# Sums of squares mostly in bf16 instead of fp32, evenly spaced covariance units and a relu square moved back to VectorE, in a fused attention and channel-mix kernel

## Chip, cores and metric

One core of a Trainium2 chip. The metric is the device time of one execution in microseconds (us). PE is the matrix engine, VectorE is DVE, ScalarE is ACT and GpSimd is POOL in the profile.

## The reference

Four batches of 6208 rows and 256 channels. A cross-covariance attention runs over the channels, and a channel mix follows it.

```python
qn = q / (norm(q, axis=1) + 1e-6);  kn = k / (norm(k, axis=1) + 1e-6)
a = softmax(kn.T @ qn / tau)               # 256 x 256 per batch
x = v @ a                                  # 6208 x 256
xk = mu_k*x + (1-mu_k)*x_prev;  xr = mu_r*x + (1-mu_r)*x_prev
out = sigmoid(xr @ w_r) * (maximum(xk @ w_k, 0)**2 @ w_v)
```

The norms need the column sums of q² and k² over all rows of a batch.

## The kernel before

The program is emitted in a fixed order, eight steps `j` for each of 48 blocks of 512 rows (12 blocks a batch). While the blocks of one batch go through the channel mix, the covariance of the next batch is made in between, in *units* of 128 rows. A unit is two matmuls, and every second unit has one ScalarE square of the q and k rows; the last unit of a batch has 64 rows. The squares are added up on VectorE. Each add is queued at build time and emitted at one of three places in a block (steps 1, 6 and 7; at step 2 too while a softmax chain waits for its sums).

Names in the views: `delta`, `xk` and `xr` mix each row with the one before it; `kr` is the relu and `kk` its square; `vr_ps` is the PSUM buffer of the last matmuls of 128 rows, and `res` the step that reads and frees it; `sq` and `acc` are squares and their sums, and `bank` holds the norms.

```python
def unit_square(b, g, s):                  # two rows (s, s+1) of a group of four
    ...
    t = pq.tile([P, 2, 2 * C], F32, name="sq2", ...)
    adds.append((now[0] + 2, b, t))
    if apart(b, g):                        # batch 1: q and k lie apart, two squares
        for i in range(2):
            nc.scalar.activation(t[:rows, :, i * C:(i + 1) * C], rows_at(qk, b, g, i)[:rows, s:s + 2], AF.Square)
    else:
        nc.scalar.activation(t[:rows], qk[...], AF.Square)

def next_add():
    _, b, t = adds.pop(0)
    nc.vector.tensor_tensor(sums[b], sums[b], t, op=OP.add)     # 128 x 1024 fp32
...
# up(): relu of each of 8 tiles on ScalarE; in blocks 1-33 ScalarE also squares the first of them
if fh == 0 and by_act(i):
    nc.scalar.activation(st[i, "kk"][:, 0, :m], kr, AF.Square)
...
# finish(): frees vr_ps, of which there are two
nc.scalar.activation(res[:, s], vr_ps[:, D:], AF.Tanh, scale=0.5)
nc.vector.scalar_tensor_tensor(res[:, s], res[:, s], 1.0, vr_ps[:, :D], op0=OP.add, op1=OP.mult)
...
# the block loop: the steps j that take a unit
elif i < 7:
    slots = (1, 2, 3, 4, 5, 7) if i < 3 else (1, 2, 3, 4, 5, 6, 7)
elif i == 7:
    slots = (1, 2, 7)
elif (i - 7) % NB == 0:
    slots = (5, 7)
else:
    slots = (1, 3, 4, 5, 7) if (i - 7) % NB in (1, 3, 6, 9) else (1, 3, 5, 7)
if j in slots and pos["mm"] < len(units):
    unit()
if adds and adds[0][0] <= now[0] and (j in (1, 6, 7) or j == 2 and adds[0][1] == holds[0] and chain):
    next_add()
```

After a batch's last unit comes its softmax `chain`, one piece a step. It holds the norms (small matmuls on the sums) back until all adds of that batch have been emitted.

Of the kernel before, what the change touches and what calls it, by code (L numbers as in the profile page):

```python
# [18 lines left out]
def kernel(  # L19
# [13 lines left out]
    nc = tc.nc  # L33
# [173 lines left out]
    def unit_square(b, g, s):  # L207

        rows, n = rows_of(b, g)
        if s % 2:  # L210
            return
        qk = groups[b, g][0]
        if n == 1:
            t = pq.tile([P, 1, 2 * C], BF16, name="sq", tag="sq1", bufs=2)
            sums[b, "left"] = t
        elif (g, s) == (1, 0):
            t = pn.tile([P, 2, 2 * C], F32, name="acc", tag="acc", bufs=2)
            sums[b] = t
        else:
            t = pq.tile([P, 2, 2 * C], F32, name="sq2", tag=f"f{s // 2}", bufs=6)  # L220
            adds.append((now[0] + 2, b, t))
        if apart(b, g):
            for i in range(2):
                nc.scalar.activation(t[:rows, :, i * C:(i + 1) * C], rows_at(qk, b, g, i)[:rows, s:s + 2], AF.Square)
        else:
            nc.scalar.activation(t[:rows], qk[:rows, s:s + min(n, 2)].rearrange("p s i c -> p s (i c)"), AF.Square)  # L226

    def next_add():
        _, b, t = adds.pop(0)
        nc.vector.tensor_tensor(sums[b], sums[b], t, op=OP.add)  # L230

    def unit_matmul(b, g, s):
        rows, n = rows_of(b, g)
# [11 lines left out]
    def softmax_pieces(b):  # L245

        s_ps = cov.pop(b) if b else None
        rn = pn.tile([P, 4], F32, name="rn")
        s_sb = pn.tile([P, 2, C], F32, name="s_sb")
        e_sb = pn.tile([P, 2, C], F32, name="e_sb", bufs=1)  # L250
        mx = pn.tile([P, 2], F32, name="mx")
        sm = pn.tile([P, 2], F32, name="sm")
        rk = rn[:, 2:4]
        def fold():
            t = pq.tile([P, 2 * C], BF16, name="sq", tag="sq", bufs=1)
            nc.vector.tensor_tensor(t, sums[b][:, 0], sums[b][:, 1], op=OP.add)
            sums[b] = t

        def norms():
            bank[b] = ps.tile([P, 4], F32, name="bank", tag="xT_ps", bufs=2)  # L260
            for t, rows in ((sums.pop((b, "left"))[:, 0], L), (sums.pop(b), P)):
                for i in range(4):
                    nc.tensor.matmul(bank[b][:, i:i + 1], t[:rows, i * P:(i + 1) * P], ones[:rows, 0:1],
                                     start=rows == L and i == 0, stop=rows == P, skip_group_check=True)

        def roots():
            nc.scalar.copy(rn, bank[b])

        def diagonals():
            dg = pn.tile([P, 2, P], F32, name="dg", tag="dg", bufs=1)  # L270
            for h in range(2):
                nc.vector.tensor_tensor(dg[:, h], cov[0][h][:, 3 * P * h:3 * P * h + P], ident_f, op=OP.mult)
            nc.vector.tensor_reduce(rn[:, 0:2], dg, axis=AX, op=OP.add)

        def root(h):
            nc.scalar.activation(rn[:, 2 * h:2 * h + 2], bank[0][:, 0:2] if h else rn[:, 0:2], AF.Sqrt)

        def invert_first(h):
            nc.vector.tensor_scalar_add(rn[:, 2 * h:2 * h + 2], rn[:, 2 * h:2 * h + 2], 1e-6)
            nc.vector.reciprocal(rn[:, 2 * h:2 * h + 2], rn[:, 2 * h:2 * h + 2])  # L280
            if h and inv_tau != 1.0:
                nc.vector.tensor_scalar_mul(rk, rk, inv_tau)

        def evac_first():
            for h in range(2):
                nc.vector.tensor_scalar_mul(s_sb[:, h], cov[0][h][:, P:P + C], rn[:, h:h + 1])

        def pow2():
            nc.gpsimd.tensor_tensor(rn, rn, half, op=OP.pow)

        def invert():
            nc.vector.tensor_scalar_add(rn, rn, 1e-6)
            nc.vector.reciprocal(rn, rn)
            for h in range(2):
                nc.vector.tensor_scalar_mul(s_sb[:, h], s_sb[:, h], rn[:, h:h + 1])
            if inv_tau != 1.0:
                nc.vector.tensor_scalar_mul(rk, rk, inv_tau)

        def evac():
            nc.scalar.copy(s_sb, s_ps)  # L300

        def turn():

            st_ps[b] = ps.tile([P, 2, C], F32, name="st_ps", tag="xT_ps", bufs=2)
            for n in range(4):
                ih, dh = divmod(n, 2) if b else (n % 2, n // 2)
                nc.tensor.transpose(st_ps[b][:, ih, dh * P:(dh + 1) * P], s_sb[:, dh, ih * P:(ih + 1) * P],  # L307
                                    ident_f)

        def exp():  # L310
            for ih in range(2):
                if not bounded:
                    nc.vector.tensor_reduce(mx[:, ih:ih + 1], st_ps[b][:, ih], axis=AX, op=OP.max, negate=True)
                    nc.vector.tensor_tensor(mx[:, ih:ih + 1], mx[:, ih:ih + 1], rk[:, ih:ih + 1], op=OP.mult)
                nc.scalar.activation(e_sb[:, ih], st_ps[b][:, ih], AF.Exp, scale=rk[:, ih:ih + 1],
                                     bias=0.0 if bounded else mx[:, ih:ih + 1],
                                     accum_out=sm[:, ih:ih + 1])

        def shares():
            nc.gpsimd.tensor_tensor(sm, sm, minus[:, 0:2], op=OP.pow)  # L320

        def weigh():
            for ih in range(2):
                nc.scalar.activation(a_sb[:, b, ih, :], e_sb[:, ih], AF.Copy, scale=sm[:, ih:ih + 1])

        def weigh_first(ih):
            nc.vector.reciprocal(sm[:, ih:ih + 1], sm[:, ih:ih + 1])
            nc.vector.tensor_scalar_mul(a_sb[:, b, ih, :], e_sb[:, ih], sm[:, ih:ih + 1])

        if b == 0:  # L330
            return diagonals, root, invert_first, evac_first, turn, exp, weigh_first

        return [evac, fold, None, None, norms, roots, pow2, None, invert, None, None, turn, exp, shares, None, weigh]



# [154 lines left out]
    def up(i, fh):  # L491
        m = size(i)
        if fh == 0:
            st[i, "kk"] = p2.tile([P, 8, M], BF16, name="kk", tag="kk", bufs=2)
        xk = st[i, "xk"]
        kT_ps = ps.tile([P, M], F32, name="kT_ps", tag="kT_ps", bufs=3)
        for dh in range(2):
            nc.tensor.matmul(kT_ps[:, :m], w_k_sb[:, dh, fh * P:(fh + 1) * P], xk[:, dh, :m],  # L498
                             start=dh == 0, stop=dh == 1)
        if fh % 4 == 0 and (i or fh):  # L500
            st[i, "kr", fh // 4] = p2.tile([P, 4, M], BF16, name="kr", tag="kr", bufs=2)
        kr = st[i, "kr", fh // 4][:, fh % 4, :m]
        nc.scalar.activation(kr, kT_ps[:, :m], AF.Relu, scale=0.5 ** 0.5)  # L503
        if fh == 0 and by_act(i):
            nc.scalar.activation(st[i, "kk"][:, 0, :m], kr, AF.Square)

    def by_act(i):
        return 1 <= i < 3 * NB - 2

    def square(i, fh):  # L510
        m = size(i)
        n = 4 if fh < 4 and i < NBLK - 1 else 2
        if fh % n == n - 1:
            lo = 1 if fh == 3 and by_act(i) else fh % 4 + 1 - n
            kr = st[i, "kr", fh // 4][:, lo:fh % 4 + 1, :m]
            nc.vector.tensor_tensor(st[i, "kk"][:, fh // 4 * 4 + lo:fh + 1, :m], kr, kr, op=OP.mult)  # L516

# [116 lines left out]
            pos["ld"] += 1  # L634

    chain = []
    FOLD = 15
    holds = [0]

    def unit(ahead=2):  # L640
# [58 lines left out]
    for i in range(-2, NBLK - 1):  # L699
        for j in range(8):  # L700
# [6 lines left out]
                v_load(i + 6)  # L707
            if chain:
                piece = chain[0]
                if len(chain) == FOLD and any(e[1] == holds[0] for e in adds):  # L710
                    piece = None
                else:
                    chain.pop(0)
                if piece is not None:
                    piece()
# [41 lines left out]
                slots = ()  # L757
            elif i == 0:
                slots = (5, 6, 7)
            elif i < 7:  # L760
                slots = (1, 2, 3, 4, 5, 7) if i < 3 else (1, 2, 3, 4, 5, 6, 7)
            elif i == 7:
                slots = (1, 2, 7)
            elif (i - 7) % NB == 0:
                slots = (5, 7)
            else:
                slots = (1, 3, 4, 5, 7) if (i - 7) % NB in (1, 3, 6, 9) else (1, 3, 5, 7)
            if j in slots and pos["mm"] < len(units):
                unit()
            if adds and adds[0][0] <= now[0] and (j in (1, 6, 7) or j == 2 and adds[0][1] == holds[0] and chain):  # L770
                next_add()
            now[0] += 1
            if i >= 0 and i % NB == 2 and j == 1 and i // NB < B:
# [41 lines left out]
```

## Time and profile before

| what | value |
|---|---|
| time, median of the first 3 runs | 510.97 us (510.47 to 512.49) |
| span of the profiled run, granted clock | 508.8 us, 0.998 |
| block 0 starts (first r matmul) | 52.4 us |

The busy shares of the profile page (engine, us, share of the span, instructions) do not separate the engines.

```profile
PE 481.0 (95%) x3382; PEld 330.3 (65%) x3441; DVE 445.2 (88%) x751; ACT 446.1 (88%) x925; POOL 99.2 (20%) x146
```

A better reading is the time of one block, from its first r matmul (`vr_ps<-w_r_sb,xr`) to that of the next. The windows view below gives, for each stretch, its length and then the busy time of each engine. Overlapping records count once here, so length minus busy time is idle time. The rows are blocks 1-9 together, block 6, block 7, block 12 (four units) and block 36 (no units).

```profile
core 0: us, PE busy (x) PEld busy (x) DVE busy (x) ACT busy (x) POOL busy (x), PEclk, DMA share, GB/s
62.36:155.43 93.07, 91.20 (x649) 62.96 (x660) 91.75 (x142) 90.53 (x202) 29.37 (x43) 1.00 1.16 180
113.52:123.86 10.34, 10.29 (x78) 7.38 (x79) 9.83 (x16) 10.28 (x25) 4.10 (x6) 1.00 1.31 218
123.86:134.98 11.12, 9.89 (x67) 6.37 (x67) 11.12 (x17) 10.15 (x22) 0.00 (x0) 1.00 1.24 191
174.77:184.32 9.55, 9.50 (x67) 6.60 (x68) 9.00 (x15) 8.89 (x20) 2.77 (x4) 1.00 1.36 210
402.82:411.50 8.68, 8.63 (x59) 5.88 (x60) 7.09 (x13) 7.06 (x16) 0.74 (x1) 1.00 0.59 120
```

Plain blocks take 8.68 us, and each unit adds 0.22 us: four units give 9.56. Blocks 1-9 are the exception. Block 7 has only three units (9.34 us by this count) and takes 11.12 us, and VectorE is busy for all of them.

Two views show what happens in block 7. The first is the list of waits of PE from 52 us on (who waited for whom, total, times, longest). The second is VectorE's timeline (start, length, operation).

```profile
PE vr_ps L531 <- DVE res L545: 1.2, 2, 0.8
```

```profile
126.39 1.21 DVE L230 TENSOR_TENSOR acc<-acc,sq 128x1024 f32<-128x1024 f32 x1
127.52 0.74 DVE L483 SCALAR_TENSOR_TENSOR xr<-delta,mu_t,xT 128x512 bf16<-128x512 bf16 x1
128.18 1.21 DVE L230 TENSOR_TENSOR acc<-acc,sq 128x1024 f32<-128x1024 f32 x1
129.32 0.41 DVE L545 SCALAR_TENSOR_TENSOR res<-res,vr_ps 128x256 f32<-128x256 f32 x1
```

The res step that frees a `vr_ps` buffer stands behind two fp32 adds of 1.21 us and an xr mix, and PE waits for it. These are the costs in question, from the groups by shape (count, then busy us and mean ns):

```profile
L230 DVE TENSOR_TENSOR acc<-acc,sq 128x1024 f32<-128x1024 f32 x69 | 83.9, 1216 | 0.0
L516 DVE TENSOR_TENSOR kk<-kr 128x1536 bf16<-128x1536 bf16 x33 | 31.3, 950 | 0.0
L505 ACT ACTIVATE kk<-kr 128x512 bf16<-128x512 bf16 x33 | 20.8, 630 | 1.1
```

### The profile page before, as it was taken

The numbers are of one execution on the slowest core, as the hardware profiler recorded it, in microseconds if no ns is written. First come the engines' busy times: TensorE is split into PE (matmuls) and PEld (weight loads), VectorE is DVE, ScalarE is ACT, GpSimd is POOL, SyncE is SP. The second block draws the span as 40 slices with busy tenths as digits, with TensorE's granted clock in tenths as the row PEclk, the third lists the DMA queues.
The fourth block names the chain that finished last, engine by engine and source line by source line (L and its number), as shares of the span: only waits on it lengthen the run. The fifth ranks groups of instructions, "written<-read, shape, count | busy, mean of one in ns | idle before, by whom it ended". The sixth has DMA issues, their size and how long they took to land. (4 is left out here: it accounts for less than half of the span.)

```text
span 508.8 us, 9277 instructions
## 1 busy us (share of the span) xinstructions
PE 481.0 (95%) x3382; PEld 330.3 (65%) x3441; DVE 445.2 (88%) x751; ACT 446.1 (88%) x925; POOL 99.2 (20%) x146
## 2 busy tenths in 40 slices
PE   4677999999899999999999999999999999999996
PEld 1344666766666666677666677667666666666675
DVE  3778899999999999999979999999878787878884
ACT  5768999999899999999899999999897878888784
POOL 0043242223053131211252132000131000000000
PEclk9999999999999999999999999999999999999999
DMA  8999999999789999997699999934496753342123
GB/s 320 410 321 199 196 178 208 173 189 219 154 147 190 194 217 155 168 191 117 113 159 193 172 193 175 183 87 104 84 189 129 151 97 103 87 88 80 47 79 104
DMA packets 131926, 83.46 MB, mean 164 GB/s; under 512 B 50660, under 2 KB 124712, under 8 KB 131880
## 3 DMA queue, kind: packets, MB, share of 16 engines
q0 software_dynamic: 55056, 33.01, 50.2%
q1 hardware_dynamic: 76504, 49.59, 41.4%
q8 instruction: 27, 0.44, 0.4%
q10 hardware_dynamic: 320, 0.26, 0.2%
q14 instruction: 19, 0.16, 0.1%
HBM read 78.71 MB, written 25.43 MB: 205 GB/s over the span
## 5 line engine op out<-in xcount | busy, mean ns | idle before, releaser
L503 ACT ACTIVATE kr<-kT_ps 128x512 bf16<-128x512 f32 (+1 forms) x390 | 232.2, 607 | 27.8 <-PE kT_ps L498 22.8
L535 PE MATMUL vr_ps<-w_v_sb,kk 128*128 128x256 bf16 x1536 | 230.9, 273 | 0.5
L498 PE MATMUL kT_ps<-xk,w_k_sb 128*128 128x512 bf16 (+1 forms) x722 | 217.6, 377 | 0.3 <-DVE xk L483 0.2
L535 PEld LDWEIGHTS <-kk 128*128 128x128 bf16 x1536 | 149.5, 98 | 58.9 <-DVE kk L516 1.1
L516 DVE TENSOR_TENSOR kk<-kr 128x1536 bf16<-128x1536 bf16 (+2 forms) x148 | 116.8, 789 | 0.2 <-ACT kr L503 0.2
L545 DVE SCALAR_TENSOR_TENSOR res<-res,vr_ps 128x256 f32<-128x256 f32 x192 | 79.6, 415 | 42.5 <-ACT res L544 42.3
L498 PEld LDWEIGHTS <-w_k_sb 128*128 128x128 bf16 x780 | 75.5, 98 | 27.5 <-issue 0.6
L230 DVE TENSOR_TENSOR acc<-acc,sq 128x1024 f32<-128x1024 f32 x69 | 83.9, 1216 | 0.0
L544 ACT ACTIVATE res<-vr_ps 128x256 f32<-128x256 f32 x192 | 76.6, 399 | 1.3 <-PE vr_ps L535 1.3
L531 PE MATMUL vr_ps<-w_r_sb,xr 128*128 128x256 bf16 x384 | 73.3, 272 | 3.8 <-DVE res L545 1.2
L483 DVE SCALAR_TENSOR_TENSOR xk<-delta,mu_t,xT 128x512 bf16<-128x512 bf16 x94 | 69.9, 744 | 0.0
L483 DVE SCALAR_TENSOR_TENSOR xr<-delta,mu_t,xT 128x512 bf16<-128x512 bf16 x94 | 69.8, 743 | 0.0
L531 PEld LDWEIGHTS <-xr 128*128 128x128 bf16 x384 | 37.6, 98 | 46.3 <-issue 2.6
L392 ACT CAST xT<-xT_ps 128x512 bf16<-128x512 f32 x94 | 55.4, 589 | 12.6 <-PE xT_ps L390 12.5
L390 PE MATMUL xT_ps<-vT,a_sb 128*128 128x512 bf16 x188 | 55.9, 379 | 1.4 <-DVE vT L375 1.4
L242 PE MATMUL s_ps<-qk 128*128 128x256 bf16 (+1 forms) x294 | 55.8, 273 | 0.0
L127 POOL DMA_DIRECT2D qk<-in_q_dram x39 | 26.1, 670 | 140.8 <-ACT kr L503 64.3
L226 ACT ACTIVATE sq<-qk 128x1024 f32<-128x1024 bf16 (+1 forms) x49 | 51.0, 1041 | 0.0
L349 POOL DMA_DIRECT2D v_bf<-in_v_dram x48 | 36.0, 752 | 48.6 <-DMA vT<-v_bf 29.0
L190 PE MATMUL s_ps<-qk 128*128 128x384 bf16 (+2 forms) x98 | 20.0, 350 | 16.1 <-ACT qk L147 15.1
L473 DVE TENSOR_TENSOR delta<-xT 128x1024 bf16<-128x1024 bf16 x47 | 32.2, 685 | 1.1 <-ACT xT L392 1.1
L242 PEld LDWEIGHTS <-qk 128*128 128x128 bf16 (+1 forms) x294 | 28.5, 98 | 5.6 <-issue 0.8
(104 smaller groups left out, 241.2 us busy)
## 6 DMA issues: line engine op xcount, KB each, us to landing
out_dram<-res SPq DMA_DIRECT2D x47, 512.0 KB, 4.0
v_bf<-in_v_dram POOLq DMA_DIRECT2D x48, 256.0 KB, 9.6
qk<-in_q_dram POOLq DMA_DIRECT2D x36, 256.0 KB, 8.5
qk<-in_k_dram POOLq DMA_DIRECT2D x36, 256.0 KB, 9.5
f<-in_q_dram SPq DMA_DIRECT2D x11, 512.0 KB, 9.4
f<-in_k_dram SPq DMA_DIRECT2D x11, 512.0 KB, 9.9
vT<-v_bf SPq DMA_TRANSPOSE x44, 5.5
f<-in_q_dram SPq DMA_DIRECT2D x2, 256.0 KB, 9.0
```

Of the source, the lines that this page charges most:

```text
L230: nc.vector.tensor_tensor(sums[b], sums[b], t, op=OP.add)
L242: nc.tensor.matmul(s_ps[:, ih, :], rows_at(qk, b, g, 0)[:rows, s, ih * P:(ih + 1) * P], rows_at(qk, b, g, 1)[:rows, s, :], start=t0 and ih ...
L390: nc.tensor.matmul(xT_ps, a_sb[:, b, ih, dh * P:(dh + 1) * P], vT[:, :, ih, :], start=ih == 0, stop=ih == 1)
L392: nc.scalar.copy(xT[:, dh, 1:], xT_ps)
L483: nc.vector.scalar_tensor_tensor(o[:, dh], st[i, "d"][:, dh], mu[:, dh:dh + 1], st[i, "x"][:, dh, :M], op0=OP.mult, op1=OP.add)
L498: nc.tensor.matmul(kT_ps[:, :m], w_k_sb[:, dh, fh * P:(fh + 1) * P], xk[:, dh, :m], start=dh == 0, stop=dh == 1)
L503: nc.scalar.activation(kr, kT_ps[:, :m], AF.Relu, scale=0.5 ** 0.5)
L516: nc.vector.tensor_tensor(st[i, "kk"][:, fh // 4 * 4 + lo:fh + 1, :m], kr, kr, op=OP.mult)
L531: nc.tensor.matmul(vr_ps[:, D:], xr[:, dh, s * P:(s + 1) * P], w_r_sb[:, dh, :], start=dh == 0, stop=dh == 1)
L535: nc.tensor.matmul(vr_ps[:, :D], kk[:, fh, s * P:(s + 1) * P], w_v_sb[:, fh, :], start=fh == 0, stop=fh == 7)
L544: nc.scalar.activation(res[:, s], vr_ps[:, D:], AF.Tanh, scale=0.5)
L545: nc.vector.scalar_tensor_tensor(res[:, s], res[:, s], 1.0, vr_ps[:, :D], op0=OP.add, op1=OP.mult)
```

## The change

The change has three parts. The squares of four rows go into one bf16 tile, are summed in pairs in bf16, and one row is added to an fp32 sum. The units are spaced evenly, six in each of blocks 1-7 and then four. The first relu square goes back from ScalarE to VectorE. The intent of the change is to relieve VectorE and ScalarE in the blocks where they are fullest.

```diff
+        if s == 0:
+            sums[b, g] = pq.tile([P, S, 2 * C], BF16, name="sq4", tag=f"f{g % 2}", bufs=6)
+        t = sums[b, g]
...        (batch 1: one square with permuted output instead of two)
+        if s == 2:
+            adds.append((now[0] + 2, b, lambda: pairs_add(b, g)))
+            adds.append((now[0] + 3, b, lambda: quad_add(b, g)))
+
+    def pairs_add(b, g):
+        t = sums[b, g]
+        nc.vector.tensor_tensor(t[:, 0:2], t[:, 0:2], t[:, 2:4], op=OP.add)
+
+    def quad_add(b, g):
+        t = sums.pop((b, g))
+        nc.vector.tensor_tensor(t[:, 0], t[:, 0], t[:, 1], op=OP.add)
...
+        nc.vector.tensor_tensor(to, sums[b], t[:, 0], op=OP.add)     # to: fp32; bf16 for the last
...
-        if fh == 0 and by_act(i):
-            nc.scalar.activation(st[i, "kk"][:, 0, :m], kr, AF.Square)
...
-            lo = 1 if fh == 3 and by_act(i) else fh % 4 + 1 - n
+            lo = fh % 4 + 1 - n
...
-            elif i < 7:
-                slots = (1, 2, 3, 4, 5, 7) if i < 3 else (1, 2, 3, 4, 5, 6, 7)
-            elif i == 7:
-                slots = (1, 2, 7)
-            elif (i - 7) % NB == 0:
-                slots = (5, 7)
-            else:
-                slots = (1, 3, 4, 5, 7) if (i - 7) % NB in (1, 3, 6, 9) else (1, 3, 5, 7)
+            elif i < 8:
+                slots = (1, 2, 3, 4, 5, 7)
+            elif (i - 8) % NB == 0:
+                slots = (3, 4, 5, 7)
+            else:
+                slots = (1, 3, 4, 5, 7) if (i - 8) % NB == 5 else (1, 3, 5, 7)
...
-            if adds and adds[0][0] <= now[0] and (j in (1, 6, 7) or j == 2 and adds[0][1] == holds[0] and chain):
+            if adds and adds[0][0] <= now[0] and (j in (1, 6, 7) or adds[0][1] == holds[0] and chain):
```

The softmax chain also loses its `fold` piece, since the sum is already one row. With the new spacing a batch's last unit falls a block later, and so does its chain.

More of the change, by code (lines that the diff above doesn't have):

```diff
@@ L213, in unit_square @@
         if n == 1:
-            t = pq.tile([P, 1, 2 * C], BF16, name="sq", tag="sq1", bufs=2)
-            sums[b, "left"] = t
-        elif (g, s) == (1, 0):
-            t = pn.tile([P, 2, 2 * C], F32, name="acc", tag="acc", bufs=2)
-            sums[b] = t
-        else:
-            t = pq.tile([P, 2, 2 * C], F32, name="sq2", tag=f"f{s // 2}", bufs=6)
-            adds.append((now[0] + 2, b, t))
-        if apart(b, g):
-            for i in range(2):
-                nc.scalar.activation(t[:rows, :, i * C:(i + 1) * C], rows_at(qk, b, g, i)[:rows, s:s + 2], AF.Square)
-        else:
-            nc.scalar.activation(t[:rows], qk[:rows, s:s + min(n, 2)].rearrange("p s i c -> p s (i c)"), AF.Square)
+            t = sums[b, "left"] = pq.tile([P, 1, 2 * C], BF16, name="sq", tag="sq1", bufs=2)
@@ new lines, in unit_square @@
+            nc.scalar.activation(t[:rows], qk[:rows].rearrange("p s i c -> p s (i c)")[:, :1], AF.Square)
+            return
+        if s == 0:
+            sums[b, g] = pq.tile([P, S, 2 * C], BF16, name="sq4", tag=f"f{g % 2}", bufs=6)
+        t = sums[b, g]
+        to = t[:, s:s + 2].rearrange("p s (i c) -> p i s c", i=2)
+        if apart(b, g):
+            nc.scalar.activation(to, qk.rearrange("p s i c -> p (s i c)").rearrange(
+                "p (i s c) -> p i s c", i=2, s=S)[:, :, s:s + 2], AF.Square)
+        else:
+            nc.scalar.activation(t[:, s:s + 2], qk[:, s:s + 2].rearrange("p s i c -> p s (i c)"), AF.Square)
@@ new lines, in unit_square @@
+        if s == 2:
[7 more added lines that the diff above has]
+        nc.vector.tensor_tensor(t[:, 0], t[:, 0], t[:, 1], op=OP.add)
+        if g == 1:
+            sums[b] = t[:, 0]
+            return
+        if g == NB:
+            to = pq.tile([P, 2 * C], BF16, name="sq", tag="sq", bufs=1)
+        elif g == 2:
+            to = pn.tile([P, 2 * C], F32, name="acc", tag="acc", bufs=2)
+        else:
+            to = sums[b]
+        nc.vector.tensor_tensor(to, sums[b], t[:, 0], op=OP.add)
+        sums[b] = to
@@ L228, in next_add @@
     def next_add():
-        _, b, t = adds.pop(0)
-        nc.vector.tensor_tensor(sums[b], sums[b], t, op=OP.add)
+        adds.pop(0)[2]()
     def unit_matmul(b, g, s):
@@ L253, in softmax_pieces @@
         rk = rn[:, 2:4]
-        def fold():
-            t = pq.tile([P, 2 * C], BF16, name="sq", tag="sq", bufs=1)
-            nc.vector.tensor_tensor(t, sums[b][:, 0], sums[b][:, 1], op=OP.add)
-            sums[b] = t
         def norms():
@@ L331, in softmax_pieces @@
             return diagonals, root, invert_first, evac_first, turn, exp, weigh_first
-        return [evac, fold, None, None, norms, roots, pow2, None, invert, None, None, turn, exp, shares, None, weigh]
+        return [evac, None, None, norms, roots, pow2, None, invert, None, None, turn, exp, shares, None, weigh]
     blocks = [(b, t) for b in range(B) for t in range(NB)] + ["left"]
@@ L503, in up @@
         nc.scalar.activation(kr, kT_ps[:, :m], AF.Relu, scale=0.5 ** 0.5)
-        if fh == 0 and by_act(i):
-            nc.scalar.activation(st[i, "kk"][:, 0, :m], kr, AF.Square)
-    def by_act(i):
-        return 1 <= i < 3 * NB - 2
     def square(i, fh):
@@ L636 @@
     chain = []
-    FOLD = 15
+    NORMS = 12
     holds = [0]
@@ L709 @@
                 piece = chain[0]
-                if len(chain) == FOLD and any(e[1] == holds[0] for e in adds):
+                if len(chain) == NORMS and any(e[1] == holds[0] for e in adds):
                     piece = None
```

## The prediction

> **What bounds it now.** From 52 us on, TensorE (PE). Its 95% busy share does not prove it: the Trainium skill ("Perfetto Trace Analysis", Identifying the Most-Contended Engine) calls matmul occupancy a poor measure. So I took block periods from the timeline (first r matmul of each 512-row block to the next): 8.68 us for blocks without covariance units; 9.56 us with four units, 9.78 with five. One unit costs PE 0.22 us. A plain block's columns, at the trace's spacing of back-to-back matmuls (about 107 ns per 256 columns), take 8.53 us: PE is within 2% of its own rate. DVE and ACT (88% busy) hide behind it, except around blocks 1-9.
>
> There, blocks 3-6 have seven units each: 3.5 fp32 adds of 1.216 us a block. DVE shows 11.0-11.5 us of (slightly overlapping) records in periods of 10.2-10.3 us, ACT 13.4-13.8. DVE runs back to back and carries a backlog into block 7. At 128.6 and 131.5 us in the timeline PE waits for the DVE res step that frees vr_ps (list of waits: 1.2 us together; in matmul spacing 1.0 and 0.5). Block 7 has three units, should take 9.34 us, and takes 11.12.
>
> **Removed, added, moved.**
> - DVE: per group of four rows two fp32 adds of 128x1024 (2.43 us) become a bf16 add of 1024 (0.685, as delta of that shape takes), one of 512 (0.42) and an fp32+bf16 add of 512 (0.68, as the fold takes): 1.78 us. The skill ("VectorE: DVE Perf Modes", perf-mode tier table) gives tensor_tensor 2x in bf16 against 1x in fp32; this trace agrees, 0.685 against 1.216 us. 36 groups save 24 us, the folds 2. The relu square of the first 512 columns comes back: (1.218 - 0.950) x 33 = 9 us. DVE: -16, to about 429 us.
> - ACT: 33 squares of 0.63 us leave (-21). Batch 1's two 0.68 us squares per pair become one of about 1.06 (24 pairs, -7). To about 418 us.
> - PE: same instructions; units six in each of blocks 1-7 instead of 6,6,7,7,7,7,3. Adds: three a block for three slots. Batch 1's softmax starts five steps later, still in time for block 12.
>
> **On the critical path.** Little. PE work is unchanged, so only PE's waits can be won: block 7 about 1.8 us, block 1 0.4, blocks 8-9 0.5, blocks 3-6 and 20-22 0.3: 3.0 us at most. The first 52 us and blocks 33-47 do not change. I take 2.7 us as won, 0.2 for some new wait.
>
> **Predicted: 508.4 us**, 8 in 10 between 506.9 and 510.2. Faster by over 2%: 1%; within 2%: 98%; slower: 1%.
>
> **What the profile would show.** DVE busy 425-433 us, ACT 414-422; blocks 2-7 each 10.0-10.1 us, block 7 no longer 11.1; no wait of a vr_ps matmul for DVE res near 130 us; four-unit blocks still 9.56 us, plain ones 8.68. If the four-unit blocks get shorter, PE was not their bound, and I am wrong about where the time lies.
>
> **What would make it wrong.** The pair, quad and accumulator adds come close together, late in a block; if they delay a res step, or the larger relu square delays kk, PE waits in every block with units (0.1 us in each of 31 would eat the gain). Batch 1's square with permuted output may take over 1.06 us. The later chain puts its transposes beside the x transposes' PSUM buffers and may cost tenths.

## The result and the profile after

The kernel after took 508.38 us, median of 4 runs (508.2 to 508.85). Before took 510.83 in the same set (4 runs, 510.47 to 512.49). The ratio is 0.9947, with a 95% interval of 0.9924 to 0.997. Ratios here are the mean time of one kernel's fast runs over that of the other's in the same rounds, so they are not quite the ratio of the medians. The gain is clear of the noise, but well under the 2% that counts as faster here. Experiment 12 repeats the kernel.

The busy shares of the page after:

```profile
PE 484.2 (95%) x3441; PEld 331.1 (65%) x3441; DVE 431.0 (85%) x784; ACT 428.4 (84%) x868; POOL 98.8 (19%) x146
```

PE's extra busy time here is not extra work. The trace of before lacks 59 of PE's matmul records.

The windows view after has the same blocks in the same order, and block 33 as a last row:

```profile
62.70:152.93 90.23, 90.23 (x658) 63.19 (x657) 83.74 (x150) 82.97 (x169) 26.77 (x40) 1.00 1.26 185
112.88:123.00 10.12, 10.12 (x78) 7.18 (x77) 9.79 (x18) 9.29 (x20) 2.93 (x5) 1.00 1.40 174
123.00:132.99 9.99, 9.99 (x74) 7.03 (x72) 9.11 (x17) 9.61 (x20) 1.48 (x2) 1.00 1.30 180
172.25:181.81 9.56, 9.56 (x70) 6.66 (x69) 8.64 (x16) 8.56 (x18) 2.23 (x3) 1.00 1.42 183
401.09:409.77 8.68, 8.68 (x61) 5.87 (x60) 7.09 (x13) 7.05 (x16) 1.44 (x2) 1.00 0.59 121
374.17:383.72 9.55, 9.28 (x65) 6.30 (x64) 7.61 (x15) 8.11 (x21) 4.96 (x7) 1.00 0.63 119
```

Blocks 1-9 fell by 2.84 us, and block 7 from 11.12 to 9.99. The four-unit block and the plain block did not move, although VectorE and ScalarE are less busy in the four-unit one. Not all of the 2.84 us is won. Before had 52 units in these nine blocks and after has 50, so 2 x 0.22 = 0.44 us is work put off. The unit of 64 rows, at which PE loses another 0.2 us, also moved from block 9 to block 10. The true gain there is 2.2 us.

PE's list of waits after, from 52 us on, has one wait for a res step. It is a new one, in block 33 at 381 us:

```profile
PE vr_ps L541 <- DVE res L555: 0.3, 1, 0.3
```

The groups that took the place of the costly ones:

```profile
L526 DVE TENSOR_TENSOR kk<-kr 128x2048 bf16<-128x2048 bf16 x48 | 58.5, 1218 | 1.1 <-ACT kr L518 1.1
L232 DVE TENSOR_TENSOR sq<-sq 128x1024 bf16<-128x1024 bf16 x36 | 24.6, 683 | 0.0
L246 DVE TENSOR_TENSOR acc<-acc,sq 128x512 f32<-128x512 f32 x27 | 18.7, 692 | 0.9
L236 DVE TENSOR_TENSOR sq<-sq 128x512 bf16<-128x512 bf16 x36 | 15.0, 417 | 0.0
```

One group of four rows costs 0.683 + 0.417 + 0.692 = 1.79 us, where it cost 2 x 1.216 = 2.43 us. The add of an fp32 and a bf16 operand (L246) takes 0.69 us for 512 elements, as long as the fold of before (0.68 us), whose two operands were fp32. The cheap part is only the adds in which every operand is bf16.

### The profile page after: what moved, and what is told of

It reads as the page before. It is cut to its first block, busy times and chain, and to the rows that moved or that the text cites. A ratio compares the mean times of both kernels' runs of the same rounds, so it can differ in the third digit from the quotient of the medians.

```text
span 507.1 us, 9288 instructions
## 1 busy us (share of the span) xinstructions
PE 484.2 (95%) x3441; PEld 331.1 (65%) x3441; DVE 431.0 (85%) x784; ACT 428.4 (84%) x868; POOL 98.8 (19%) x146
## 4 chain that ended last, share of the span: by engine, by line
PE 87%; DMA 5%; DVE 4%; ACT 2%; SPq 0%; issue 0%; DVEq 0%
PE vr_ps L545 32%; PE kT_ps L513 31%; PE vr_ps L541 8%; PE xT_ps L405 8%; PE s_ps L262 6%; DMA f<-in_k_dram 5%; DVE kk L526 1%; DVE vT L390 1%; DVE xk L498 1%; ACT xT L407 0%; PE s_ps L190 0%; ACT kr L518 0%; PE y_ps L583 0%; PE x_ps L429 0%; ACT qk L147 0%; PE st_ps L322 0%
## 5 line engine op out<-in xcount | busy, mean ns | idle before, releaser
L513 PE MATMUL kT_ps<-xk,w_k_sb 128*128 128x512 bf16 (+1 forms) x780 | 230.0, 377 | 0.2 <-DVE xk L498 0.2
L526 DVE TENSOR_TENSOR kk<-kr 128x2048 bf16<-128x2048 bf16 (+1 forms) x148 | 125.7, 849 | 1.3 <-ACT kr L518 1.3
L225 ACT ACTIVATE sq<-qk 128x1024 bf16<-128x1024 bf16 x48 | 50.9, 1061 | 0.0
L262 PEld LDWEIGHTS <-qk 128*128 128x128 bf16 (+1 forms) x294 | 28.5, 98 | 5.6 <-issue 0.8
L190 PEld LDWEIGHTS <-qk 128*128 128x128 bf16 (+1 forms) x98 | 10.1, 105 | 25.9 <-issue 14.8
```

Source lines behind the costliest of these rows:

```text
L225: nc.scalar.activation(t[:, s:s + 2], qk[:, s:s + 2].rearrange("p s i c -> p s (i c)"), AF.Square)
L262: nc.tensor.matmul(s_ps[:, ih, :], rows_at(qk, b, g, 0)[:rows, s, ih * P:(ih + 1) * P], rows_at(qk, b, g, 1)[:rows, s, :], start=t0 and ih ...
L513: nc.tensor.matmul(kT_ps[:, :m], w_k_sb[:, dh, fh * P:(fh + 1) * P], xk[:, dh, :m], start=dh == 0, stop=dh == 1)
L526: nc.vector.tensor_tensor(st[i, "kk"][:, fh // 4 * 4 + lo:fh + 1, :m], kr, kr, op=OP.mult)
```

## The experiments

My theory was that VectorE's adds made PE wait in blocks 1-9, and that PE's own rate bounds the rest. The rivals were that the new spacing alone did it, that ScalarE was the one that held these blocks, and that VectorE sets the pace elsewhere too. Twelve kernels ran, in three sets. All were correct.

### 1. The spacing alone

The kernel before with only the new `slots` of the diff above.

> The kernel before with only the new spacing of the covariance units (six a block in blocks 1-7, then four). Own theory: PE waits come where VectorE falls behind; with three fp32 adds instead of three and a half, VectorE has about 7.64 + 3 x 1.216 = 11.3 us of records a block, less about 1.4 us of overlap, so 9.9 us for a period of 10.0: just enough, most of the gain, 508.9 us (508.4 to 509.8), block 7 near 10.0-10.3 us. Rival (cheaper adds are the cause): no gain, 510.5 or more.

Measured: 509.0 us (508.87 to 509.25), before 510.64, ratio 0.9957 (0.9933 to 0.9982). Blocks 1-9 in the windows view:

```profile
62.32:153.53 91.21, 90.34 (x646) 62.56 (x657) 90.91 (x141) 89.48 (x200) 27.06 (x40) 1.00 1.25 182
```

The spacing alone gives 1.6 us, of the 2.2 us that experiment 4 shows in the same set. VectorE has only 0.3 us idle in these blocks, against 1.3 us in before, and its busy time is 0.8 us shorter, because the two units put off take an add with them, less overlap. So the fp32 adds nearly fit when they come evenly, but with nothing to spare.

### 2. The cheaper sums alone

The kernel after with the old `slots`, and with the first relu square back on ScalarE.

> The kernel after with the old spacing (seven units in blocks 3-6) and the first relu square back on ScalarE: only the bf16 squares and sums are new. Own theory: a seven-unit block has about 7.64 + 1.75 x 1.78 = 10.75 us of VectorE records, less about 1.4 of overlap, 9.4 us for a period of 10.22: no backlog, so block 7 falls from 11.1 us to about 9.5 and the total is 508.4 us (508.0 to 509.2). Rival (the spacing alone is the cause): no gain, 510.5 or more.

Measured: 511.66 us (510.35 to 512.85), before 510.64, ratio 1.0013 (0.9981 to 1.0044): no gain. Even its fastest run, 510.35 us, only equals the fastest of before. My expectation was wrong. VectorE was not short, since it was busy for only 83.54 of the 93.41 us of blocks 1-9. The list of waits of this run has a new entry instead, and VectorE's timeline shows what PE waited for:

```profile
PE bank L278 <- DVE sq L246: 2.5, 1, 2.5
```

```profile
128.18 0.69 DVE L232 TENSOR_TENSOR sq<-sq 128x1024 bf16<-128x1024 bf16 x1
128.78 0.95 DVE L531 TENSOR_TENSOR kk<-kr 128x1536 bf16<-128x1536 bf16 x1
129.65 0.74 DVE L498 SCALAR_TENSOR_TENSOR xk<-delta,mu_t,xT 128x512 bf16<-128x512 bf16 x1
130.31 0.42 DVE L236 TENSOR_TENSOR sq<-sq 128x512 bf16<-128x512 bf16 x1
130.77 0.69 DVE L246 TENSOR_TENSOR sq<-acc,sq 128x512 bf16<-128x512 f32 x1
```

PE reached the norm matmuls of batch 1 at 129 us. The last add of the batch had been emitted just one step ahead of them, and ran from 130.77. Seven units a block queue 3.5 adds, and the program emits three. The leftover adds went out at the end, in front of the norms. This is a debt in the order of emission, which gives a second theory. Experiment 9 tests it.

### 3. The relu square alone

In the kernel before:

```diff
-        return 1 <= i < 3 * NB - 2
+        return False
```

> The kernel before with only the first relu square moved from ScalarE to VectorE. Own theory: 0.27 us more for VectorE in each block, which was already behind in blocks 3-7, so the backlog grows by over 1 us and the time goes up: 511.9 us (511.0 to 513.0). Rival (ScalarE, at 13.4-13.8 us of records a block, was what held blocks 3-7): the time falls by 0.5 us or more, to 510.2 or less.

Measured: 512.82 us (512.67 to 513.14), before 510.64, ratio 1.0033 (1.0008 to 1.0058). Blocks 1-9:

```profile
62.63:156.68 94.05, 91.51 (x648) 62.48 (x658) 93.69 (x141) 86.90 (x192) 28.85 (x43) 1.00 1.17 176
```

ScalarE was relieved by 3.6 us there, VectorE took 1.9 us more, and the blocks took 1.0 us longer. So VectorE held them and not ScalarE, although both were nearly full. Three of the eight waits for a res step in this run lie after 160 us, where before has none: block 14 takes 9.84 us instead of 9.56. With this square on top VectorE sets the pace in some later blocks too.

### 4. The relu square back on ScalarE, in the kernel after

```diff
+        if fh == 0 and by_act(i):
+            nc.scalar.activation(st[i, "kk"][:, 0, :m], kr, AF.Square)
```

> The kernel after with the first relu square back on ScalarE in blocks 1-33. Own theory: with VectorE and ScalarE both inside the block period, this part of the change is worth nothing: 508.4 us (508.0 to 509.0), PE periods unchanged, VectorE 9 us less busy and ScalarE 21 us more. Rival (the move is part of the gain): 509 us or more.

Measured: 508.44 us (507.96 to 509.83), before 510.64, ratio 0.9949 (0.9923 to 0.9975), the same as the kernel after. Once the sums are cheap and the units evenly spaced, where this square stands costs nothing.

### 5 and 6. More VectorE work, and more PE work, in blocks 10-31

The same `delta` made twice, and (another kernel) one up matmul made twice. The results are unchanged.

```diff
+            for _ in range(2 if 10 <= i < 32 else 1):
                 nc.vector.tensor_tensor(delta, xT[:, :, 1:], xT[:, :, :M], op=OP.subtract)
```
```diff
+            if dh == 0 and fh == 6 and 10 <= i < 32:
+                nc.tensor.matmul(kT_ps[:, :m], w_k_sb[...], xk[:, dh, :m], start=True, stop=True)
             nc.tensor.matmul(kT_ps[:, :m], w_k_sb[...], xk[:, dh, :m], start=dh == 0, stop=dh == 1)
```

> The kernel after with the delta subtraction done twice in blocks 10 to 31: 22 x 0.685 = 15 us more work for VectorE, same result. Theory (PE is the bound there, the other engines only hide): four-unit blocks have 9.7 + 0.7 = 10.4 us of records less about 1.4 overlap, inside 9.56: time within 0.4 us of the kernel after. Rival (VectorE sets the pace): 8 us or more longer.

> The kernel after with one matmul of 512 columns repeated in each of blocks 10 to 31, same result: 22 x 0.213 = 4.7 us more for PE at the spacing of the trace. Theory: all of it comes through, 4.2 to 5.2 us longer (512.6 to 513.6), each of those blocks 0.21 us longer. Rival (PE has slack in those blocks): under 2 us longer.

The PE one took 513.87 us (513.05 to 514.55), 5.5 us over the kernel after (which ran in another set; the split kernel of experiment 7, in this set, took 508.19). Each of the blocks concerned grew by 0.21 us (block 12 from 9.56 to 9.77), 4.6 us over 22 blocks. Block 0 of the profiled run also started 1.0 us later, in a stretch that the edit does not touch. PE has no slack in these blocks.

The VectorE one took 514.04 us (513.83 to 514.35), 5.7 us over the kernel after (508.38): neither theory's number. The four-unit blocks took 9.81 to 9.89 us, and VectorE still had idle time in each, as the windows row of block 16 shows. VectorE's timeline there, and PE's line for the matmul that follows the second res, show why:

```profile
212.38:222.27 9.89, 9.72 (x69) 6.64 (x68) 9.33 (x17) 8.45 (x18) 2.94 (x5) 1.00 1.02 158
```

```profile
215.74 0.42 DVE L556 SCALAR_TENSOR_TENSOR res<-res,vr_ps 128x256 f32<-128x256 f32 x1 [0.49 <-ACT res L555]
216.07 1.41 DVE L489 TENSOR_TENSOR delta<-xT 128x1024 bf16<-128x1024 bf16 x2
217.40 1.22 DVE L527 TENSOR_TENSOR kk<-kr 128x2048 bf16<-128x2048 bf16 x1
218.54 0.75 DVE L499 SCALAR_TENSOR_TENSOR xk<-delta,mu_t,xT 128x512 bf16<-128x512 bf16 x1
219.20 0.41 DVE L556 SCALAR_TENSOR_TENSOR res<-res,vr_ps 128x256 f32<-128x256 f32 x1
```

```profile
219.67 0.38 PE L542 MATMUL vr_ps<-w_r_sb,xr 128*128 128x256 bf16 x2 [0.17 <-DVE res L556]
```

VectorE idles 0.49 us before one res, because it waits for ScalarE's tanh. It then has the delta (twice), a relu square and an xk mix to do before the next res, which frees PE's buffer. The idle time before the first res was not used for the second delta: VectorE ran its operations in the order in which the program emits them. This is the one matmul of block 16 that starts late. This gave a third theory: the place in the order counts, not the total.

### 7 and 8. The new wait of block 33, and a wait before block 0

In block 33 of the kernel after, the 1.22 us relu square of block 34 starts late and stands before the res that PE waits for, as VectorE's timeline shows. In matmul spacing (from the start of one matmul to the next, less the usual time of its columns) PE loses 0.43 us.

```profile
379.07 1.22 DVE L526 TENSOR_TENSOR kk<-kr 128x2048 bf16<-128x2048 bf16 x1 [0.37 <-ACT kr L518]
380.21 0.74 DVE L498 SCALAR_TENSOR_TENSOR xk<-delta,mu_t,xT 128x512 bf16<-128x512 bf16 x1
380.87 0.41 DVE L555 SCALAR_TENSOR_TENSOR res<-res,vr_ps 128x256 f32<-128x256 f32 x1
```

The first edit splits that one square; the second kernel has both edits.

```diff
-        n = 4 if fh < 4 and i < NBLK - 1 else 2
+        n = 4 if fh < 4 and i < NBLK - 1 and i != 34 else 2
```
```diff
-                v_transpose_pe(i + 3, nc.vector.tensor_copy)()
+                v_transpose_pe(i + 3, nc.scalar.copy if i < 0 else nc.vector.tensor_copy)()
```

> The kernel after with the first relu square of block 34 done as two halves, so that a short one and not the 1.22 us one stands before the res step that PE waited for at 381 us (0.43 us in matmul spacing). Theory: block 33 falls from 9.55 to about 9.11 us and the time by 0.4 us, to 508.0 (507.7 to 508.3). Rival (another step holds that res, such as the exp pair on ScalarE): no change.

> As the run with the split square, and the copy of the PE-transposed values of block 2 out of PSUM moved from VectorE to ScalarE, which is idle there while PE waits 1.36 us for that copy just before block 0. Theory: block 0 starts about 1.1 us earlier, time 506.9 us (506.4 to 507.6), better than both kernels. Rival (the step after it waits for something else, or ScalarE is late as well): no more than 0.3 us gained over the split alone.

The split took 508.19 us (508.14 to 508.34), ratio to before 0.9927 (0.9902 to 0.9952). Block 33 fell as expected:

```profile
374.01:383.13 9.12, 9.12 (x66) 6.31 (x65) 7.79 (x16) 8.00 (x21) 4.60 (x7) 1.00 0.62 121
```

A shorter square thus removes the wait. But its length is only part of the cause. The square of block 34 is just as long in before and in the kernel of experiment 1, and there PE waits for no res in block 33. Their lines, before first:

```profile
380.77 1.22 DVE L516 TENSOR_TENSOR kk<-kr 128x2048 bf16<-128x2048 bf16 x1
378.77 1.22 DVE L516 TENSOR_TENSOR kk<-kr 128x2048 bf16<-128x2048 bf16 x1
```

In both it follows the delta without a gap. In the kernel after it starts 0.37 us late, because it waits for a relu, and on ScalarE the last relus stand behind the two exps of batch 3's softmax chain:

```profile
377.52 0.48 ACT L330 ACTIVATE e_sb<-st_ps,rn 128x256 f32<-128x256 f32 x1
377.97 0.48 ACT L330 ACTIVATE e_sb<-st_ps,rn 128x256 f32<-128x256 f32 x1
378.42 1.10 ACT L518 ACTIVATE kr<-kT_ps 128x512 bf16<-128x512 f32 x2
```

In experiment 1, whose chain still has its fold, the exps come one relu later (378.29), and block 33 takes 9.12 us with the whole square. So by the traces the moved chain made the square late, and the exp pair, the rival of the expectation, is part of the cause. No run moved the exps alone, so this part is argued and not shown.

The whole time moved by only some 0.2 us between medians of different sets, which is no more than the medians of the kernel after itself differ (508.38 and 508.82). Both edits together took 507.38 us (506.96 to 507.95), ratio 0.9915 (0.9884 to 0.9945): the fastest kernel. In its profile block 0 starts at 50.9 us instead of 52.7, and PE's 1.36 us wait for that copy is gone. Runs of before in this set spread widely (510.25 to 513.35, median 511.89), so the medians of the variants tell more than these ratios: 507.38 against 508.19 us, 0.8 of the 1.1 us expected.

### 9 and 10. A fourth place for the adds

Experiment 2 with one more place for a queued add, in front of a res step for which VectorE idles; and the kernel before with the same.

```diff
-            if adds and adds[0][0] <= now[0] and (j in (1, 6, 7) or ...
+            if adds and adds[0][0] <= now[0] and (j in (1, 2, 6, 7) or ...
```

> The run with the adds alone and the old spacing of units, with one more place a block where a queued add may be emitted (step 2, before a res step for which VectorE idles). In the run before, PE waited 2.5 us for the last sum of batch 1, although VectorE had idled 0.9 to 1.3 us in each of blocks 3-6: three places a block do not empty a queue that grows by three and a half. New theory (the order of emission cost it, not VectorE's capacity): that wait falls under 0.3 us, block 7 is near 9.5 us, and the time is 508.6 us (508.0 to 509.3). Rival (seven units a block are too many by themselves): 510.0 or more.

> The kernel before with the same fourth place for its fp32 adds. Theory (before is short of VectorE time in blocks 1-8, where VectorE has no idle time in the trace): a place more does not help, since the work is the same: 510.6 us (510.0 to 512.0), the wait only moves. Rival (before too lost its time to the order of emission alone): 509.0 or less.

The first took 508.29 us (508.18 to 508.58), before 510.58, ratio 0.9953 (0.994 to 0.9965). Block 7 takes 9.73 us, and PE has no listed wait in blocks 1-33. So cheap sums on the *old* spacing give the whole gain, once they are emitted in time. The second took 510.69 us (510.54 to 510.87), ratio 0.9997 (0.9985 to 1.0009). Blocks 1-9 of these two, in that order:

```profile
62.16:153.03 90.87, 90.24 (x650) 63.42 (x661) 83.18 (x153) 88.76 (x182) 29.28 (x43) 1.00 1.29 184
```

```profile
62.16:155.42 93.26, 91.53 (x650) 62.98 (x661) 91.32 (x140) 91.33 (x202) 29.43 (x43) 1.00 1.29 182
```

With fp32 adds the fourth place only moved the loss: blocks 4 and 6 grew to 10.8 us each and block 7 fell to 10.5. In the windows view of that run VectorE is busy for all of blocks 6 and 7. (In before it is not, as my expectation has it, without idle time: block 6 has 0.5 us of it.) The adds' order cost the cheap version, their size cost the fp32 version.

### 11. More VectorE work where VectorE idles

In the kernel after, the second xr mix made twice in blocks 10-31, just before the res for which VectorE waits.

```diff
+            for _ in range(2 if key == "xr" and dh and 10 <= i < 32 else 1):
                 nc.vector.scalar_tensor_tensor(o[:, dh], st[i, "d"][:, dh], mu[:, dh:dh + 1], ...)
```

> The kernel after with a 0.74 us VectorE operation (the second xr mix, same result) done twice in each of blocks 10 to 31, just before the res step for which VectorE idles about 0.9 us a block. It is more added work (16 us) than the doubled delta (15 us), which cost 5.6 us because it stood between two res steps with no idle time before the second. New theory (what counts is where in VectorE's order the work stands): within 0.5 us of the kernel after, 508.4 (508.0 to 508.9). Rival (VectorE's total is at its limit in these blocks): 5 us or more longer.

Measured: 508.32 us (508.12 to 508.62), before 510.58, ratio 0.9951 (0.9939 to 0.9964). This is more added work than in experiment 5, and it costs nothing. Its block 16, in the windows view:

```profile
210.17:219.72 9.55, 9.45 (x67) 6.65 (x68) 9.38 (x17) 8.44 (x18) 2.94 (x5) 1.00 1.03 148
```

VectorE is busy 9.38 of 9.55 us, more than in experiment 5, and the block is as short as ever.

### 12. Control

The kernel after again, on the same chip and in the same rounds as 9 to 11.

> The kernel after, unchanged, as a control on the same chip in the same rounds: 508.4 us (508.1 to 508.9) by every theory.

Measured: 508.82 us (508.17 to 513.71), ratio 0.9975 (0.9947 to 1.0004). One of its six runs took 513.71 us and pulls the mean. The other five lie between 508.17 and 509.35.

## Why the prediction was right, and where a step of it was not

- **The time.** 508.4 us was forecast and 508.38 measured. "Little on the critical path" held: unchanged block times of 9.56 and 8.68 us, and the PE experiment, in which every added 0.21 us came through. The agreement to 0.02 us is luck: the same kernel had a median of 508.82 in another set, and some terms of the sum were off.
- **The won waits.** 3.0 us at most was forecast, 2.7 taken. The profiles show 2.5: 2.2 from blocks 1-9, of which block 7 gave 1.8 as forecast, and 0.3 from blocks 19-22 (39.55 us before, 39.26 after, with 16 units and one chain's matmuls in both). The 0.5 forecast for blocks 8-9 was mostly no waiting: batch 1's norm matmuls and transposes stood in block 8, and in the kernel after the same work makes blocks 8 and 9 take 9.94 and 9.99 us instead of 9.56.
- **The new wait.** I allowed 0.2 us, and named a larger relu square, and the later chain for its PSUM buffers. A wait of 0.43 us came, in block 33 alone. The square in it was no larger than before. The chain did matter, but through its exps on ScalarE (experiment 7). That the allowance was near is luck.
- **The step that failed: "3.5 fp32 adds a block ... DVE runs back to back and carries a backlog into block 7".** Counted in the timeline, blocks 3-6 run three adds each, because the program has three places. VectorE even idles 0.5 us in block 6 (10.34 - 9.83). The backlog was of adds not yet emitted. It fell on block 7, which runs four adds: the one at 128.18, in front of the res that PE waits for, stands at step 2, which is open because batch 1's chain waits. There PE had the fewest units to do. Two things were therefore needed: cheaper adds, or for most of the gain an even spacing, for VectorE's time, and an order that emits the adds early enough. The change has both. Its sums without the spacing gave nothing (experiment 2), and with one more place they gave everything (experiment 9).
- **"DVE and ACT hide behind it"** is true of the kernel as it stands, but not because of free time as such. 15 us more VectorE work in one place cost 5.7 us, 16 us more in another cost nothing.
- **ScalarE's share** fell to 428 us, not to 418. The term was mis-sized because I subtracted record lengths from a busy total in which overlaps count once. Added record by record, ScalarE's records went from 528.0 to 497.8 us, 30 less, near the forecast 28. The busy total fell by 17.7, because the packed records of before overlapped more. VectorE's 431 us lay inside the forecast.
- **The duration of the squares.** The Trainium skill ("ScalarE: Activation LUTs", What ACT_TABLE_LOAD costs) says that an activation runs at one element a cycle and lane, "fp32 and bf16 alike". The square of 1024 elements took 1066 ns with an fp32 output and 1061 with a bf16 one. The bf16 tile helped VectorE alone.

## What to carry to other kernels

When one engine is at its own rate, a saving on another is worth only the waits it removes, so look for the blocks that are longer than their work and read what stands before the releasing instruction. Where an engine runs its work in the order of emission, as VectorE did in these timelines, ask where the slack is and not how much: 16 us of work in front of an idle spot were free here, and 15 us between two releases cost 5.7 us. When work is queued at build time, count how many items a block makes and how many it emits, and see which block inherits the rest.

## What the Trainium skill lacked or had wrong

- "Perfetto Trace Analysis", Identifying the Most-Contended Engine, calls occupancy a fair measure of how close VectorE is to its roofline. Here it did not tell whether added work costs time: a four-unit block with VectorE busy 9.38 of 9.55 us lost nothing, and one with it busy 9.33 of 9.89 us had lost 0.33 us. The page has nothing on slack by place in the order.
- "VectorE: DVE Perf Modes", perf-mode tier table, has columns for bf16, for fp32 and for PSUM operands, and none for mixed types. A mixed add (fp32 sum plus bf16 row, 512 elements) took 692 ns, against 417 for all bf16. The page's list of what the hardware checks ("every tensor is 16-bit") implies this, but gives no figure. The table's bf16 and fp32 columns agree: 683 against 1216 ns for 1024 elements.
